# Gated linear attention into a SwiGLU feed-forward block: the input layout of one early attention unit, the queue of three loads, and the places of two weight sums

## The chip, the cores and the metric

The kernel runs on one core of a Trainium2 chip. The core has a matrix engine (TensorE, PE in the profile), a vector engine (VectorE, DVE), an engine for functions of one operand (ScalarE, ACT), GpSimd (POOL) and SyncE (SP), which mostly issues transfers. The engines run their own instruction streams in order and wait for each other by semaphores. Transfers go through 16 DMA engines; the queue of SP and that of GpSimd both feed them. The metric is the device time of one execution in microseconds (us), as the median of some runs.

## What is computed

Inputs q, k, v and f_logit have the shape (4, 8, 768, 48): batch, heads, sequence, head dimension. All is float32. The first part is a recurrence over the sequence, for each batch and head:

```
f = 1 / (1 + exp(-f_logit))
state = 0                                     # 48 x 48
for t in range(768):
    state = f[t][:, None] * state + outer(k[t], v[t])
    y[t]  = q[t] @ state
```

The result is put together to 3072 tokens of 384 features (8 heads of 48), and goes through a feed-forward block with a hidden width of 1536:

```
g   = x @ w_gate
out = (g * sigmoid(g) * (x @ w_val)) @ w_out
```

## The kernel before

**Chunks and units.** The sequence is cut into 6 chunks of 128 steps. A unit is one chunk of one batch element, all 8 heads; unit u = 4c + b is chunk c of batch element b, so that units 4 to 7 are chunk 1. In a unit the recurrence becomes matrix work: VectorE forms running products of the gates, forward and backward (two scans, lines 620 and 648), and multiplies k and q by them (line 570, `kT` and `qT`); PE forms the scores (`sc`, line 666), VectorE masks them (line 681), PE forms the output `y` (lines 702 and 706, or 727) and the state's increment `dS` (line 747). `attention(u)` is a Python generator; each `next` emits the next step.

**Two ways to bring in f, k and q.** All three are needed with the head dimension on the partitions and time along the row, and are stored the other way round.
- By TensorE: one DMA of 192 KB for each of f, k, q puts time on the partitions (`raw`, line 454, SP's queue), and PE turns it by four transposes of 128x128 each (`transposed`, line 587). ScalarE reads f from PSUM with the sigmoid, VectorE reads k and q from PSUM in the multiplications.
- By squares: four DMAs of 96 KB each lay the tensor out in squares of 32x32 (`rooms`, line 447), ScalarE applies the sigmoid to f in SBUF (line 595), and VectorE turns f, k and q by one STREAM_TRANSPOSE each (lines 604, 614 and 652). PE does nothing for these. In chunk 1 the rooms are the same memory as the two slots of `raw`; there is one room each for f, k and q, so the next unit's f is loaded when this unit's f has been turned, and so on (`load_after`).

`by_squares(u)` decides. Here it holds for the last two units of chunk 1 (6 and 7) and all of the later chunks. In chunk 1 the square loads are issued from GpSimd's queue, in a fixed order (`by_pool`); in later chunks from SP's.

**Feed-forward work.** While the attention of chunk 1 runs, the feed-forward block of chunk 0 runs in its plain form (`mlp_plain`): products of 128x512 with w_gate and w_val, and then the product with w_out (`downs_abreast`, line 825). Beside it the weights, which are stored with 64-bit floats, come in by 768 KB pieces and are made into float32 (`sizes` on ScalarE, lines 488 and 490; `join` on VectorE, lines 496 to 501). From chunk 1 on the feed-forward block uses forms with fewer products: for the first two products (`mlp_fifteen`) a triple of tiles takes 15 products in place of 18 (line 1004; four triples a chunk), and for the product with w_out (`down_seven`) seven block products in place of eight (lines 1103 and 1166). VectorE adds and subtracts the results (lines 905 and 908) and forms the hidden values h (line 956). These forms need sums of weights beforehand. Those of w_out's halves are four instructions of 128x1152 on VectorE (`down_weight_sums`, line 936), of which the first two give the operands `ws`.

**What sets the order.** The main order is that in which the Python code emits instructions. Up to line 1271 it is fixed engine by engine (`in_order`); between there and line 1292 the tile framework's scheduler may move instructions, so that attention, weights and products of chunk 0 are mixed by it; from line 1298 on the order is fixed again, and steps of attention and weight sums are put in by a written clock: each product counts 0.86, each part of the product with w_out 1.95, and an entry of `waiting` comes when the clock `now` has passed its number. `DOWN_SUMS_AT` (line 901) holds the numbers of the four sums of w_out's halves; `whole`, the length of chunk 1 on that clock, is 78.9. The first sum of the four is read by the second, the second by the fourth.

**The step that loads unit 5.** Before, line 1268 (`load(B + 1)`) issues the 192 KB loads of f, k, q and v of unit 5 on SP's queue, between pieces of the weights. For unit 6 the load is issued within the attention of unit 5, when PE's transposes of k and q have been emitted (line 628).

Of the kernel before, what the change touches and what calls it, by code (L numbers as in the profile page):

```python
# [290 lines left out]
def short_path(ctx, tc, ident, least, judge, q, k, v, f_logit, moe_w_gate, moe_w_val, moe_w_out, out):  # L291
# [9 lines left out]
    nc = tc.nc  # L301
    B, H, S, D = q.shape
# [13 lines left out]
    SQUARES = 2  # L316
# [82 lines left out]
    rooms = {nm: t.rearrange("p n h w -> p (n h w)")[:, 0:Q + HP * RUN] for nm, t in both_raw.items()}  # L399

    def by_squares(u):
        return u >= SQUARES * B - 2

    def make_rooms(pool):
        for nm in "fkq":
# [3 lines left out]
    def v_of(u):  # L409
        return vs[u % (NV if units[u][1] < SQUARES else NV // 2)]  # L410
# [20 lines left out]
    def load(u, what="fkqv"):  # L431
        b, c = units[u]
        rows = slice(c * C, (c + 1) * C)
        inputs = dict(f=f_logit, k=k, q=q, v=v)
        for nm in "fqkv" if c >= SQUARES else "fvkq" if by_squares(u) else "fkqv":
            src = inputs[nm]
            if nm not in what:
                continue
            if nm == "v":
                dst = v_of(u)  # L440
            elif not by_squares(u):
                dst = raw[nm][u % NRAW]
            else:
                since = len(traced)
                for n in range(4):
                    at = Q * (1 - n % 2)
                    (nc.sync if c >= SQUARES else nc.gpsimd).dma_start(
                        out=rooms[nm][Q * n:Q * (n + 1), at:at + HP * RUN].rearrange("t (a e) -> t a e", a=HP),
                        in_=src[b, n // 2::2, rows, :].rearrange("a (t i) d -> t a (i d)", i=NI))
                if c < SQUARES:  # L450
                    by_pool.extend(ins for ins in traced[since:] if ins.engine == mybir.EngineType.Pool)
                    keep_order(by_pool[-5:])
                continue
            nc.sync.dma_start(out=dst[:, :, 0:D], in_=src[b, :, rows, :].rearrange("h t d -> t h d"))

    def weight_piece(dst, src, parts):

# [97 lines left out]
    def attention(u):  # L555
# [4 lines left out]

        diagonal = None
        in_squares = by_squares(u)

        def multiply(out, x, by):
# [60 lines left out]
        if not in_squares:  # L625
            kp = transposed("kTp", kr)
            qp = transposed("qTp", qr)
            if by_squares(u + 1):
                load(u + 1)
# [120 lines left out]
        if c >= SQUARES and u + 2 < len(units):  # L750
            load(u + 2, "v")
# [7 lines left out]
    def load_after(u, what):  # L759

        if u + 1 < len(units) and u + 1 != SQUARES * B:
            load(u + 1, what)
# [16 lines left out]
    def keep_order(mine):  # L779
        for a, b in zip(mine, mine[1:]):  # L780
            tc.add_manual_dep(b, a.name, mybir.DependencyInfo(mybir.DependencyClass.NoSync,
                                                              mybir.DependencyReason.DATA), reason="order")
# [115 lines left out]
        return {"o": banks_o, "A": banks_a}[kind].tile([128, 512], FP32, tag=kind, name="sc")  # L898

    FINISH = (3, 5, 6, 7, 9, 10)  # L900
    DOWN_SUMS_AT = (28, 34, 38, 48)
    sums = {}

    def plus(dst, a, b):
# [31 lines left out]
    def down_weight_sums():  # L936

        DH = DM // 2
        b11, b12 = w_out[:, 0:NP, 0:DH], w_out[:, 0:NP, DH:DM]
        b21, b22 = w_out[:, NP:NF, 0:DH], w_out[:, NP:NF, DH:DM]  # L940
        for i in (1, 2, 4):
            down_sums[i] = comb.tile([128, NP, DH], FP32, tag=f"ws{i}", name=f"ws{i}")
        return [lambda: minus(down_sums[1], b12, b11), lambda: minus(down_sums[2], b22, down_sums[1]),
                lambda: minus(b12, b22, b12), lambda: minus(down_sums[4], b21, down_sums[2])]
# [256 lines left out]
    def weights():  # L1201
        if fetches:
            fetches.pop(0)()
        if sizes:
            sizes.pop(0)()
        if joins:
            joins.pop(0)()
# [57 lines left out]
    joins.pop(0)()  # L1265
    hidden[1]()
    weights()
    load(B + 1)
    hidden[2]()
    steps.pop(0)()  # L1270
    in_order(mark, (mybir.EngineType.PE, mybir.EngineType.DVE, mybir.EngineType.Activation, mybir.EngineType.SP))
# [37 lines left out]

    waiting += [(at, f) for at, f in zip(DOWN_SUMS_AT, down_weight_sums())]  # L1310
    blocks = {}
# [26 lines left out]
def kernel(  # L1338
# [22 lines left out]
    def judge(bank):  # L1361
# [13 lines left out]
        yield  # L1375

    short_path(tc, ident, least, judge, *args)
    with tc.If(redo[0] > 0, label="redo"):
        general_path(tc, *args)
# [32 lines left out]
```

## Time and profile before

| | |
|---|---|
| median of 3 runs | 604.13 us (604.05 to 604.21) |
| the profiled execution's own time | 605.36 us |
| its span, from the first to the last instruction | 603.5 us |
| TensorE's mean granted clock | 0.995 |
| PE busy | 591.9 us, 98% |
| DVE busy | 480.3 us, 80% |
| ACT busy | 294.8 us, 49% |
| POOL busy | 86.2 us, 14% |

Busy time of a PE whose matmuls are pipelined is not work at its peak; where PE really waits is seen in the waits and in the distance between successive groups of the timeline. In the timeline a group's first number is its start and its second its length, and lengths of neighbouring groups overlap a little. The stages in the profile: attention of chunk 0 up to 30 us; plain feed-forward of chunk 0 with the attention of chunk 1 from 30 to 143 us; then five blocks of four triples and a product with w_out, the first of them from 143 to 240 us.

### The profile page before, as it was taken

What the parts mean: (1) busy time and instruction counts of PE and PEld (TensorE: products, weight loads), DVE (VectorE), ACT (ScalarE), POOL (GpSimd) and SP (SyncE); (2) the same over time, 40 slices, a digit from 0 to 9 for tenths busy, and PEclk for the clock granted to TensorE, in tenths of its full rate; (3) what the DMA queues carried; (4) which work ended last, traced back from release to release, by engine and by line L of the source; (5) the groups of instructions that cost most, each with busy time, mean ns of one, the idle gap of its engine ahead of it and who ended that gap; (6) DMA issues with size and microseconds to landing.
All of it is one profiled execution on the core that took longest, in us unless ns stands there. A gap on an engine that the chain in (4) does not pass through costs nothing.

```text
span 603.5 us, 10851 instructions
## 1 busy us (share of the span) xinstructions
PE 591.9 (98%) x4004; PEld 487.6 (81%) x4004; DVE 480.3 (80%) x831; ACT 294.8 (49%) x559; POOL 86.2 (14%) x199
## 2 busy tenths in 40 slices
PE   7899999999999999999999999999999999999996
PEld 5754545667888899888899888899988899988896
DVE  7999997868999977998895978995878982666631
ACT  2577853215776521567631476742376730356600
POOL 1001251000030150030330030330030320000000
PEclk9999999999999999999999999999999999999999
DMA  9998682015322044342434333343240100100001
GB/s 197 243 294 286 199 211 63 5 35 157 80 63 69 17 129 124 102 114 65 115 103 109 116 91 71 87 110 101 85 105 26 28 9 6 53 1 1 1 1 55
DMA packets 105210, 56.28 MB, mean 93 GB/s; under 512 B 67136, under 2 KB 97216, under 8 KB 105152
## 3 DMA queue, kind: packets, MB, share of 16 engines
q1 hardware_dynamic: 97632, 46.49, 29.4%
q0 software_dynamic: 5504, 6.30, 3.5%
q10 hardware_dynamic: 2016, 2.75, 1.3%
q8 instruction: 32, 0.52, 0.4%
q14 instruction: 26, 0.21, 0.1%
HBM read 45.74 MB, written 6.82 MB: 87 GB/s over the span
## 4 chain that ended last, share of the span: by engine, by line
PE 93%; DVE 5%; issue 1%; ACT 0%; DVEq 0%; ACTq 0%
PE o L1103 19%; PE A L1004 16%; PE B L1004 13%; PE c L1004 5%; PE o L1004 5%; PE gate L802 5%; PE o L825 5%; PE val L802 5%; PE sc L666 4%; PE o L1166 3%; PE y L706 3%; PE y L727 2%; PE dS L747 2%; PE y L702 2%; PE kt L670 1%; DVE c L908 1%
## 5 line engine op out<-in xcount | busy, mean ns | idle before, releaser
L717 POOL DMA_DIRECT2D xT<-yT x120 | 59.9, 507 | 50.3 <-ACT yT L710 45.3
L1103 PE MATMUL o<-w_out,h 128*128 128x192 f32 x360 | 62.0, 327 | 0.5 <-DVE h L956 0.5
L1004 PE MATMUL A<-xs,w_both 128*128 128x256 f32 x240 | 62.2, 382 | 0.0
L1103 PEld LDWEIGHTS o<-w_out,h 128*128 128x128 f32 x360 | 58.7, 190 | 1.7 <-DVE h L956 0.8
L1009 ACT COPY c<-A 128x512 f32<-128x512 f32 x40 | 23.3, 583 | 59.5 <-PE A L1004 59.5
L1009 ACT COPY aside<-A 128x512 f32<-128x512 f32 x60 | 35.1, 586 | 33.7 <-PE A L1004 33.6
L905 DVE TENSOR_TENSOR c<-c,aside 128x512 f32<-128x512 f32 x60 | 41.1, 685 | 12.4 <-ACT aside L1009 11.0
L1004 PEld LDWEIGHTS A<-xs,w_both 128*128 128x128 f32 x240 | 44.9, 190 | 6.6
L956 DVE TENSOR_TENSOR h<-h,c 128x256 f32<-128x256 f32 x100 | 40.4, 412 | 7.3 <-ACT h L1020 7.1
L681 DVE TENSOR_TENSOR A<-sc,causal 128x512 f32<-128x512 f32 x48 | 30.9, 686 | 16.9 <-PE sc L666 16.9
L908 DVE TENSOR_TENSOR c<-c,aside 128x512 f32<-128x512 f32 x60 | 40.9, 682 | 2.8 <-ACT aside L1009 2.8
L1020 ACT ACTIVATE h<-c 128x256 f32<-128x256 f32 x100 | 39.2, 416 | 7.6 <-DVE c L905 5.7
L656 POOL MEMSET gates<- 128x4 f32 x24 | 3.3, 139 | 272.6 <-DVE qT L570 267.5
L1103 PE MATMUL o<-ws,h 128*128 128x192 f32 x240 | 41.5, 328 | 0.2 <-DVE A L681 0.2
L1004 PE MATMUL B<-xs,w_both 128*128 128x256 f32 x160 | 41.3, 380 | 0.1
L1004 PE MATMUL c<-xT,w_both 128*128 128x256 f32 x160 | 41.2, 380 | 0.1
L1004 PE MATMUL A<-xs,extra 128*128 128x256 f32 x160 | 41.2, 380 | 0.0
L1004 PE MATMUL B<-xT,extra 128*128 128x256 f32 x160 | 41.1, 379 | 0.0
L1009 ACT COPY aside<-B 128x512 f32<-128x512 f32 x60 | 35.1, 585 | 9.5 <-PE B L1004 6.6
L1103 PEld LDWEIGHTS o<-ws,h 128*128 128x128 f32 x240 | 39.1, 190 | 0.8 <-DVE A L681 0.4
L905 DVE TENSOR_TENSOR c<-c,o 128x384 f32<-128x384 f32 x15 | 8.3, 552 | 36.3 <-PE o L1103 36.3
L908 DVE TENSOR_TENSOR c<-o,c 128x512 f32<-128x512 f32 x40 | 27.4, 684 | 11.0 <-ACT h L1020 6.2
(149 smaller groups left out, 1221.0 us busy)
## 6 DMA issues: line engine op xcount, KB each, us to landing
fsquares<-in_f_logit_dram SPq DMA_DIRECT2D x64, 96.0 KB, 2.5
qsquares<-in_q_dram SPq DMA_DIRECT2D x64, 96.0 KB, 2.1
ksquares<-in_k_dram SPq DMA_DIRECT2D x64, 96.0 KB, 2.4
v<-in_v_dram SPq DMA_DIRECT2D x24, 192.0 KB, 2.7
w<-in_moe_w_gate_dram SPq DMA_DIRECT2D x6, 768.0 KB, 6.1
w<-in_moe_w_val_dram SPq DMA_DIRECT2D x6, 768.0 KB, 6.2
w<-in_moe_w_out_dram SPq DMA_DIRECT2D x6, 768.0 KB, 5.6
out_dram<-ob ACTq DMA_DIRECT2D x14, 192.0 KB, 2.0
```

Of the source, the lines that this page charges most:

```text
L666: nc.tensor.matmul(sc[par][:, a * C:(a + 1) * C], lhsT=kT[r, a, :], rhs=qT[r, a, :], start=True, stop=True)
L681: nc.vector.tensor_tensor(A[:, par], sc[par].rearrange("p (a t) -> p a t", t=C), causal.unsqueeze(1).broadcast_to((128, HP, C)), ALU.mult)
L717: (nc.gpsimd if c >= SQUARES else nc.sync).dma_start(out=xT[c][f % 128:f % 128 + n, f // 128, b * C:(b + 1) * C], in_=yT[r:r + n, par, a / ...
L802: nc.tensor.matmul(p, lhsT=w[:, j, i, :], rhs=xT[c][:, i, :], start=(i == 0), stop=(i == KT - 1))
L825: nc.tensor.matmul(p, lhsT=hidden_tile(h, n // 2)[:, n % 2 * 2 + b // 2, b % 2 * C:(b % 2 + 1) * C], rhs=w_out[:, j, :], start=(n == 0), s ...
L905: nc.vector.tensor_tensor(dst, a, b, ALU.add)
L908: nc.vector.tensor_tensor(dst, a, b, ALU.subtract)
L956: lagging.append(lambda: f(*args))
L1004: nc.tensor.matmul(p[name][:, n, :], lhsT=weights_of[a][:, n, j, :], rhs=tokens[b], start=fresh and n == 0, stop=True, skip_group_check=True)
L1009: nc.scalar.copy(t, p[name])
L1020: nc.scalar.activation(dst, src[:, 0, :], AF.Silu)
L1103: nc.tensor.matmul(p[:, n, :], lhsT=lhsTs[j][:, n * C:(n + 1) * C], rhs=rhs[:, j, :], start=first and j == order[0] and n == 0, stop=j == ...
```

## The change

Three edits:
- `by_squares` holds for unit 5 too, so that three of chunk 1's four units come in by squares. Line 1268 goes: unit 5's load is now issued within the attention of unit 4, when PE's transposes of its k and q have been emitted.
- In chunk 1 the loads of v for the units by squares (5, 6 and 7) are issued from GpSimd's queue in place of SP's.
- The first two of the sums of w_out's halves come at 13.1 and 26.5 on the written clock, in place of 28 and 34. The other two stay.

```diff
     def by_squares(u):
-        return u >= SQUARES * B - 2
+        return u >= SQUARES * B - 3
...
-            nc.sync.dma_start(out=dst[:, :, 0:D], in_=src[b, :, rows, :].rearrange("h t d -> t h d"))
+            queue = nc.gpsimd if c < SQUARES and by_squares(u) else nc.sync
+            queue.dma_start(out=dst[:, :, 0:D], in_=src[b, :, rows, :].rearrange("h t d -> t h d"))
...
-    DOWN_SUMS_AT = (28, 34, 38, 48)
+    DOWN_SUMS_AT = (13.1, 26.5, 38, 48)
...
     weights()
-    load(B + 1)
     hidden[2]()
```

SQUARES and B are 2 and 4. In the instruction streams of the changed kernel PE loses twelve transposes (four each of f, k and q of unit 5), VectorE gains three STREAM_TRANSPOSEs and has the two sums in other places, SP loses four loads of unit 5 and two of v, and GpSimd's stream is, for chunk 1: v of units 5, 6 and 7, then four loads each of f, k and q of unit 5, then of unit 6, then of unit 7, with the small memsets of line 656 between. ScalarE has unit 5's sigmoid on SBUF, right after the second SiLU of line 812, with a load of its function table before it and another for the next SiLU; its number of table loads is the same.

## The prediction

> **What bounds the kernel now.** I read the chain that ended last first, then PE's waits, then the timelines of PE, VectorE and ScalarE from 143 to 207 us, where the two moved sums lie, and from 30 to 143 us, where unit 5 lies.
>
> The page's chain:
>
> ```profile
> PE 93%; DVE 5%; issue 1%; ACT 0%; DVEq 0%; ACTq 0%
> ```
>
> PE sets the end nearly everywhere. An instruction taken from PE's stream is worth its full time if nothing else becomes late, and what PE waits for is the 5%. PE's waits over 143 to 240 us name VectorE twice:
>
> ```profile
> PE o L1103 <- DVE h L956: 0.5, 1, 0.5
> PE o L1103 <- DVE A L681: 0.2, 1, 0.2
> ```
>
> The list is not complete: small waits show only as a distance between starts. PE's timeline, start and length (lines left out):
>
> ```profile
> 174.68 1.03 PE L1004 MATMUL A<-xs,w_both 128*128 128x256 f32 x4
> ...
> 187.77 1.03 PE L1004 MATMUL A<-xs,w_both 128*128 128x256 f32 x4
> 188.91 1.13 PE L1004 MATMUL B<-xs,w_both 128*128 128x256 f32 x4
> ...
> 195.30 1.13 PE L1004 MATMUL c<-xT,w_both 128*128 128x256 f32 x4
> ...
> 201.59 2.76 PE L1103 MATMUL o<-w_out,h 128*128 128x192 f32 x16
> 204.90 1.57 PE L1103 MATMUL o<-w_out,h 128*128 128x192 f32 x8 [0.55 <-DVE h L956]
> 206.39 0.67 PE L702 MATMUL y<-qT,decayed 48*64 48x128 f32 x16
> ```
>
> Triple 3 takes 13.09 us (174.68 to 187.77), triple 4 takes 13.82 (to 201.59), the first part of the product with w_out 4.80 (to 206.39). In chunk 2, which has no w_out sums, the same pieces take 13.19 (287.31 to 300.50) and 3.90 (300.50 to 304.40). So PE loses 0.63 + 0.90 = about 1.5 us here. The chain says to whom: from 174.3 to 188.3 us it runs over VectorE, both moved sums in it.
>
> ```profile
> 172.20 0.68 DVE L905 TENSOR_TENSOR c<-c,aside 128x512 f32<-128x512 f32 x1
> 174.29 1.29 DVE L681 TENSOR_TENSOR A<-sc,causal 128x512 f32<-128x512 f32 x2 [1.41 <-PE sc L666]
> ...
> 176.15 1.35 DVE L908 TENSOR_TENSOR ws<-w_out 128x1152 f32<-128x1152 f32 x1
> ...
> 185.92 1.33 DVE L908 TENSOR_TENSOR ws<-w_out,ws 128x1152 f32<-128x1152 f32 x1
> ```
>
> VectorE idles 1.41 us before 174.29, then is full (31.34 of 32 us between 175 and 207), and ScalarE waits 1.53 us for it at 188.28.
>
> From 30 to 143 us PE has no wait. VectorE is nearly full up to 99 us, but early: its h multiplications (line 816) free the PSUM banks of `val` some 4.5 us or more before PE wants them, weight tiles are joined 5.8 us or more before their first product, and between 100 and 107 us it idles 1.03, 1.89 and 2.91 us.
>
> **What the Trainium skill says.** "DMA: Bandwidth & Descriptors", section "SWDGE vs HWDGE vs iDMA": loads from GpSimd have their descriptors built in software, into rings in SBUF that VectorE can lock GpSimd out of, and each DMA engine takes turns between the queues. The same page, "Anatomy of one DMA — SWDGE (gpsimd) path": about 2.0 us plus bytes/436e3 to landing, so 2.2 us for 96 KB, and many descriptors can be made before their cost shows. Here the f loads from GpSimd landed in a median of 6.7 us, k in 2.5: the estimate is right for quiet queues, wrong where weights stream. "Perfetto Trace Analysis", "DMA Instruction — SWDGE (GPSIMD)": the profile's end is when descriptors are written, not when data has landed; so I count landing apart. "ScalarE: Activation LUTs", "What ACT_TABLE_LOAD costs": 1283 ns a load; the trace has 1.28 us (the drain that the page adds is not separate in it).
>
> **The change, part by part.**
>
> *PE's transposes.* Twelve go: unit 5's fTp delays the next group from 57.25 to 57.69 (0.44), kTp and qTp from 72.83 to 73.71 (0.88). Sum 1.32 us, on the path. PE's stream around is otherwise the same.
>
> *VectorE's three transposes.* f 1.10 us (line 604), k and q 0.70 each (614, 652), less some 0.08 overlap each: 2.3 us more in 47 to 100 us. I added up the changed kernel's VectorE stream with the before row's steps (0.46 to 0.50 for a weight step, 0.87 for a join, 0.60 for a 128x512 sum, 1.14 a scan): unit 5's f is turned at about 50, its k at 56, q at 65; the `val` banks come free 4 to 9 us before they are wanted; VectorE reaches the last h multiplication at about 100.3, where PE, 1.32 us earlier than before, delivers at 102.1 to 102.4. So it is hidden, by the idle time at 100 to 107 us; without that cover it would cost 2.3 us.
>
> *ScalarE.* Same number of table loads. But the one for unit 5's sigmoid now stands in ScalarE's queue at 40.5 us, after the SiLU at 39.96, and waits for unit 5's f. Behind it: the copy `least`, the weight steps of the next piece, a table load, the SiLUs of gate tiles 2 and 3. When does f land? GpSimd's queue: v of unit 5 after dS of unit 1 and the memset at 20.34; v of unit 6 after dS at 24.6; v of unit 7 after dS of unit 3, 30.7; f after PE's fTp of unit 4, 34.1. Four f loads at 0.55 us (line 447) end at 36.4; landing 6.7 us later gives 43. A v load has 1024 pieces of 192 bytes against 128 of 768 in an f load; no row shows it from this queue. Bounds: 0.55 us (cost per DMA) to 4.4 us (eight times as many pieces). At 4.4, v of unit 7 ends at 35.1 and f lands at 44. I take the lower value; the difference is 1 us. With 43: sigmoid done at 44.9, weight step at 46.8, table and SiLU at 48.6, whose bank PE wants at 54.2. VectorE's next weight step needs ScalarE's at 46.8 and would come at 47.2 anyway. For unit 6, f is issued when unit 5's is turned (51), lands by about 60, ScalarE arrives at 59.3, SiLUs end near 63.5, bank wanted at 67.1. Cost 0. The cover is gone when unit 5's f lands after some 47 us; from there each us is a us on PE.
>
> *SP.* It loses six loads, so weight pieces are asked for up to 5 us earlier; they were early already. Worth 0, but they share the DMA engines with f (6.7 us rather than 2.2 is for that).
>
> *Unit 5's scores.* Before, its qT was ready 1.4 us before PE's `sc` at 78.95; now about 66.6 against 77.6. Worth 0.
>
> *The two sums.* In the changed order the first stands between the last c sum of triple 1's backlog (ends 157.09) and STREAM_TRANSPOSE f at 157.94, where VectorE idles 0.84 us; the second right before the mask at 174.29, in the idle 1.41. Each takes 1.27. The first pushes the rows behind it by about 0.43 until 172.9; ScalarE's copy of c at 166.23, which waits for an h of VectorE, leaves its bank 0.5 us before PE's product at 167.34, so PE loses 0 to 0.45, I take 0.1. The second fits, leaving the mask 0.2 late. After 176 VectorE has 2 x 1.27 = 2.5 us less to do, is 2.3 us earlier at the end of triple 3, and its inputs there (asides copied by 184 to 188 us) are ready that early. The h that PE waited for at 204.41 comes up to 2 us earlier against PE; 0.55 to 1 is needed. Gain: the 1.5 us lost in triple 4 and the part after it, of which 1.1 to 1.55 is plausible; I take 1.55. The wait at 221.96 (0.19, a mask) stays. The sum kept at 48 stays late in triple 4, but with 0.8 us of slack.
>
> *Sum.* 603.5 - 1.32 - 1.55 + 0.1 = 600.7 us of span. The profiled execution took 605.36 with 1.9 us around the span and 1.2 over the median; I carry the difference, 2.77 us, to the median: 604.13 - 2.77 = 601.4 us.
>
> **Rivals.**
> - *Only the transposes count.* VectorE stays behind in triples 3 and 4 since its backlog is remade by the table loads on ScalarE or by the sum at 48, or the first sum costs its 0.45. For it: VectorE is 98% busy there. Against: chunk 2 runs the same triple without loss. 604.13 - 1.32 to 604.13 - 1.6 + 0.45: about 602.8.
> - *VectorE becomes the bound before 103.* The 2.3 us are not absorbed, PE waits for banks at the start of the product with w_out. For: full up to 99 us. Against: 5.8 us idle after it. Loses up to 2.3: 601.4 + 2.3 = 603.7, no change.
> - *Slower: ScalarE stands at unit 5's f.* Mechanism: a load in GpSimd's queue behind v, in the time of the heaviest weight traffic (DMA share 0.92 between 30 and 57 us); ScalarE is in order, and weight steps and SiLUs wait behind. It decides from landing at 47 us: a landing at 52 costs 5 us: 601.4 + 5 = 606.4. For: landing times reached 7.8 us. Against: f would have to land 13 us after its issue at 34.1.
> - That the change doesn't do what it says is excluded by the instruction streams.
>
> **How the numbers follow.** The full gain 0.62, with its own range 600.9 to 602.2; only transposes 0.15 (602.2 to 603.4); VectorE bound 0.09 (603 to 604.5); slower 0.12 (605.4 up); more gain than reckoned 0.02. The measurement tells about 0.2%, 1.2 us: faster is under 602.92, slower over 605.34. Faster 0.62 + 0.02 + 0.6 of 0.15 and a rest = 0.75; same 0.13; slower 0.12. Range for 8 in 10: 600.7 to 604.0, which takes in the full gain, the transposes alone and half of VectorE's case.
>
> **What would show it.** Right: the first product of chunk 1 (143.03 before) starts at 141.7; ScalarE's wait for f ends before 45 us; triple 4 takes 13.1 to 13.2 us and the part after it 3.9; no `ws` between 176 and 190 us. Wrong: a PE wait for ScalarE's SiLU or for VectorE's h between 54 and 106 us; a triple 2 longer than 13.36 us by more than 0.2; v loads of several us in GpSimd's rows.

## The result: 602.3 us, and where it differs from the forecast

The changed kernel takes 602.3 us in the median (601.79 to 604.62), the kernel before 604.11 us measured beside it (603.92 to 604.30). The ratio is 0.9977, 95% interval 0.9970 to 0.9983. So it is faster by 1.8 us, where 601.4 us, faster by 2.77, were forecast. The profiled execution took 602.8 us, its span is 601.1 us.

The page's chain after the change; shares of the span by engine. They add up to 86% because the chain is followed back only to 82.5 us:

```profile
PE 84%; DVE 2%; ACT 0%; issue 0%; DVEq 0%; ACTq 0%
```

PE's waits from 25 to 240 us of the changed kernel (us in total, times, longest):

```profile
PE y L728 <- ACT kt L680: 1.0, 1, 1.0
PE gate L803 <- ACT h L813: 0.9, 1, 0.9
...
PE o L1104 <- DVE A L682: 0.2, 1, 0.2
```

The 0.5 us for VectorE's `h` in the product with w_out are gone. The row for a SiLU of ScalarE is new, and the 1.0 us at `y` were 0.6 in the kernel before. Both cost time between 25 and 92 us, the stage that was to give only a gain.

PE's timeline (start, length, line, operation) at the places that the prediction named. Lines of the changed kernel are numbered one higher here than the same lines before, and in some variants a few higher still:

```profile
141.68 1.03 PE L1005 MATMUL A<-xs,w_both 128*128 128x256 f32 x4
...
173.32 1.03 PE L1005 MATMUL A<-xs,w_both 128*128 128x256 f32 x4
...
186.41 1.03 PE L1005 MATMUL A<-xs,w_both 128*128 128x256 f32 x4
...
199.50 4.33 PE L1104 MATMUL o<-w_out,h 128*128 128x192 f32 x24
203.75 0.67 PE L703 MATMUL y<-qT,decayed 48*64 48x128 f32 x16
```

Triple 3 takes 13.09 us as before, triple 4 13.09 (before 13.82), the first part of the product with w_out 4.25 (before 4.80). The moved sums return 0.73 + 0.55 = 1.28 us. VectorE's timeline shows the four sums, and the idle time that is left beside them:

```profile
155.66 1.35 DVE L909 TENSOR_TENSOR ws<-w_out 128x1152 f32<-128x1152 f32 x1
171.64 1.34 DVE L909 TENSOR_TENSOR ws<-w_out,ws 128x1152 f32<-128x1152 f32 x1
176.18 0.69 DVE L909 TENSOR_TENSOR c<-o,c 128x512 f32<-128x512 f32 x1 [1.31 <-PE o L1005]
190.67 1.35 DVE L909 TENSOR_TENSOR w_out<-w_out 128x1152 f32<-128x1152 f32 x1
197.21 1.34 DVE L909 TENSOR_TENSOR ws<-w_out,ws 128x1152 f32<-128x1152 f32 x1
```

Chunk 1 starts at 141.68 us, as forecast (141.7), against 143.03. But that agreement is an accident. The profiled execution of before had something that is no part of the kernel: a dip of PE's clock just ahead of the chunk's first weights. Stretches 26 to 31 us of the two profiles (columns: stretch, length, busy time and instructions of PE, weight loads, VectorE, ScalarE, GpSimd, then PE's clock, DMA share, GB/s); the first line is of before, the second of after:

```profile
26.00:31.00 5.00, 4.36 (x65) 3.54 (x62) 4.86 (x12) 2.31 (x7) 0.00 (x0) 0.70 0.91 217
```

```profile
26.00:31.00 5.00, 3.97 (x67) 2.67 (x64) 4.83 (x12) 2.99 (x8) 0.73 (x2) 1.00 1.02 263
```

PE's mean clock is 0.70 in one and 1.00 in the other. By single microseconds the first isn't an even 0.70: the clock is 0.50 from 28 to 31 us and 0.81 over the next, so that it was halved for 3.4 us. One of these rows of before:

```profile
29.00:30.00 1.00, 1.00 (x21) 0.62 (x14) 0.97 (x3) 0.29 (x1) 0.00 (x0) 0.50 0.71 209
```

The dip comes in some executions, of the kernel before as of variants of both. The kernel with only the sums moved, below, shows what it costs: its profiled execution has the dip too (0.70) and took 604.03 us. Four of its 16 executions took 604.03 to 604.44 us at a mean clock of 0.996, the other twelve 602.67 to 603.01 at 0.998 or more. That is 1.3 us, and in the traces 1.35 (the first `val` product starts at 34.09 us in before, at 32.74 in a kernel without the dip and without the costs told below). It also accounts for the 1.2 us by which the profile of before lay over its median. Without it chunk 1 of the kernel before would start at 143.03 - 1.35 = 141.68 us. (The kernel with only v moved, below, agrees: no dip, PE 0.23 us late at 29.85 us, chunk 1 at 141.91.) So in this execution of the changed kernel nothing at all is left of the 1.32 us of transposes.

### The profile page after: what moved, and what is told of

It reads as the page before. It is cut to its first block, busy times and chain, and to the rows that moved or that the text cites. A ratio compares the mean times of both kernels' runs of the same rounds, so it can differ in the third digit from the quotient of the medians.

```text
span 601.1 us, 10842 instructions
## 1 busy us (share of the span) xinstructions
PE 588.2 (98%) x3992; PEld 484.8 (81%) x3992; DVE 482.1 (80%) x834; ACT 294.8 (49%) x559; POOL 95.3 (16%) x214
## 4 chain that ended last, share of the span: by engine, by line
PE 84%; DVE 2%; ACT 0%; issue 0%; DVEq 0%; ACTq 0%
PE o L1104 20%; PE A L1005 18%; PE B L1005 14%; PE o L1005 6%; PE c L1005 6%; PE o L826 5%; PE sc L667 3%; PE o L1167 3%; PE y L707 2%; PE y L728 1%; PE y L703 1%; PE dS L748 1%; PE gate L803 1%; PE val L803 1%; PE kt L671 0%; DVE A L682 0%
## 5 line engine op out<-in xcount | busy, mean ns | idle before, releaser
L1005 PEld LDWEIGHTS A<-xs,w_both 128*128 128x128 f32 x240 | 44.9, 190 | 6.6
```

Source lines behind the costliest of these rows:

```text
L1005: nc.tensor.matmul(p[name][:, n, :], lhsT=weights_of[a][:, n, j, :], rhs=tokens[b], start=fresh and n == 0, stop=True, skip_group_check=True)
```

## What took it: two rows of the trace

**A SiLU behind a weight step.** In chunk 0's feed-forward block PE forms the twelve `gate` tiles in order, after the first two in pairs, and the last pair (tiles 10 and 11) goes into PSUM banks that the SiLUs of tiles 8 and 9 have to free. PE's wait for the SiLU of tile 8 is called the wait at gate tile 8 below. PE at that place, and ScalarE's timeline ahead of it, in the changed kernel:

```profile
91.65 5.42 PE L803 MATMUL gate<-xT,w_both 128*128 128x512 f32 x12 [0.86 <-ACT h L813]
```

```profile
86.53 0.56 ACT L680 COPY kt<-kt 128x512 f32<-128x512 f32 x1
88.60 1.09 ACT L489 ACTIVATE up<-w 128x768 uint16<-128x768 uint32 x1 [1.50 <-DVE w_both L502]
89.70 1.28 ACT L813 ACT_TABLE_LOAD   x1
91.00 0.60 ACT L813 ACTIVATE h<-gate 128x512 f32<-128x512 f32 x1
```

ScalarE's weight step `up` of a w_out piece writes into a buffer that VectorE's join of w_both (87.61 to 88.56) frees. ScalarE is in order, so the table load and the SiLU of gate tile 8, whose bank PE wants at 90.79, stand behind it. The same rows of the kernel before:

```profile
86.87 1.08 ACT L488 ACTIVATE up<-w 128x768 uint16<-128x768 uint32 x1 [4.61 <-DVE w_both L501]
87.81 0.58 ACT L812 ACTIVATE h<-gate 128x512 f32<-128x512 f32 x1
```

The wait was there already and longer, 4.61 us. It cost nothing: the SiLU was done at 88.39 and PE wanted the bank at 93.01 (91.66 without the dip). In the changed kernel the join starts 1.72 us later (87.61 against 85.89), a table load of 1.28 us has come in between (unit 7's sigmoid now stands at 83.83, before the SiLUs of tiles 8 and 9, not at 92.74 behind them), and PE is there earlier.

**A v load that holds VectorE.** GpSimd's and VectorE's timelines of the changed kernel around the second moved v load, and PE's `y` behind them:

```profile
24.95 0.89 POOL L455 DMA_DIRECT2D v<-in_v_dram  x1 [2.90 <-PE dS L748]
```

```profile
25.27 0.73 DVE L497 TENSOR_SCALAR top<-top 128x384 f32<-128x384 f32 x1
...
27.40 1.28 DVE L682 TENSOR_TENSOR A<-sc,causal 128x512 f32<-128x512 f32 x2
```

```profile
28.19 1.21 PE L728 MATMUL y<-A,v 128*32 128x128 f32 x32 [1.02 <-ACT kt L680]
```

The same TENSOR_SCALAR and `y` in the kernel before (the length of `y` there is stretched by the dip):

```profile
25.27 0.35 DVE L496 TENSOR_SCALAR top<-top 128x384 f32<-128x384 f32 x1
```

```profile
27.80 1.84 PE L727 MATMUL y<-A,v 128*32 128x128 f32 x32 [0.64 <-issue]
```

In the changed kernel the step ends at 26.00, 0.16 us after GpSimd is done at 25.84. Everything behind it on VectorE is 0.38 us late, the mask A (now 27.40, before 27.02) too, and PE's `y`, which needs the mask, starts at 28.19 instead of 27.80. The profile puts PE's wait down to the copy of `kt`, but that had ended at 27.84; the other operand is the mask, in two instructions of 0.68 us, and the first ends at 28.08. The trace lists PE's weight load for this `y` among those that waited for the mask. The Trainium skill, "SBUF — State Buffer", section "Who interferes with whom", has the rule: VectorE in a 2-port mode and GpSimd share a pair of SBUF ports, and whoever starts first has them for the whole instruction while the other stands. `tensor_scalar` is among the operations it names as able to enter such a mode. The trace fits, if "whole instruction" is counted from a little after the start of GpSimd's row. At the third v load one VectorE step still gets through and the next is held:

```profile
30.31 0.90 POOL L455 DMA_DIRECT2D v<-in_v_dram  x1 [4.26 <-PE dS L748]
```

```profile
30.37 0.35 DVE L497 TENSOR_SCALAR top<-top 128x384 f32<-128x384 f32 x1
30.76 0.60 DVE L499 TENSOR_SCALAR top<-top 128x384 int32<-128x384 int32 x1
```

In all traces of this case 13 TENSOR_SCALAR steps are stretched beside a v load, and each ends 0.15 to 0.16 us after the load's row; a step that starts 0.05 or 0.06 us after the row's start takes its usual 0.35 us. Which mode a step ran in, the profile doesn't show.

## The experiments

The experiments ask three things: are the two parts of the change independent; does the v load cost what the two rows suggest; and is the SiLU's lateness that of VectorE's join. Lowest and highest times are given beside medians, since times of one kernel spread by up to 3 us: from the small margin at the SiLU, and from PE's clock.

**Only the sums moved** (the kernel before, no other edit):

```diff
-    DOWN_SUMS_AT = (28, 34, 38, 48)
+    DOWN_SUMS_AT = (13.1, 26.5, 38, 48)
```

> The kernel before with the two w_out sums moved and nothing else. Theory A (the change is two independent parts, and triple 4 and the part after it lost their time to the two sums): triple 4 takes 13.1 instead of 13.82 us, the first part of the product with w_out 4.25 instead of 4.80, chunk 1 starts as before (143.0), no wait of PE between 54 and 107 us; 1.28 us off, about 602.8. Rival B (the stalls go with VectorE's earlier arrival in chunk 1, that is with the transposes): triple 4 stays at 13.8 us and the time at about 604.1.

602.83 us (602.67 to 604.44), ratio 0.9982 (0.9975 to 0.9990). Triple 4 takes 13.08 us, the part after it 4.28, and PE's wait for `h` there is gone. Theory A holds: 1.28 us in the trace, 1.23 in the medians, come from the sums alone. That chunk 1 starts at 143.05 us, as expected, is again the dip, which this execution has as before had.

**Only the units** (the changed kernel with the sums where they were):

```diff
-    DOWN_SUMS_AT = (13.1, 26.5, 38, 48)
+    DOWN_SUMS_AT = (28, 34, 38, 48)
```

> The changed kernel with the sums where they stood before: unit 5 by squares and v from GpSimd's queue alone. Theory A: PE loses twelve transposes (1.32 us) and waits 0.86 us for a SiLU near 91.6, chunk 1 starts 0.46 us earlier than in the kernel before, triple 4 stays at 13.8 and the part after it at 4.8 us; about 603.65. Rival B (the stalls go with the transposes): triple 4 near 13.1 us and about 602.4. Rival C (no new wait here, the wait in the changed kernel is of the sums): about 602.8.

603.64 us (603.03 to 604.37), ratio 0.9991 (0.9982 to 0.9999). Triple 4 is back at 13.83 us, the wait of 0.55 for `h` too, and PE waits 0.48 us at gate tile 8. So unit 5 by squares, with v from GpSimd's queue, is worth 0.4 us in place of 1.32. The time is what theory A gave (603.65), but not for its reason: it counted one loss of 0.86 us, where the trace has two, 0.48 at gate tile 8 and 0.38 from the v load.

**All v loads back in SP's queue** (the changed kernel otherwise):

```diff
-            queue = nc.gpsimd if c < SQUARES and by_squares(u) else nc.sync
+            queue = nc.sync
```

> The changed kernel with its v loads put back in SP's queue; VectorE's and ScalarE's order as in the changed kernel. Theory A (the queue of the v loads is worth nothing): f of unit 5 lands at 43 to 44 us, the wait for the SiLU near 91.6 stays between 0.6 and 1.1 us, the time is that of the changed kernel (602.3) within 0.3. Rival D (the v loads share the DMA engines with f and weights from GpSimd's side, and make VectorE's weight steps late): f lands earlier, the SiLU's wait shrinks below 0.4 us, about 601.7.

601.25 us (601.10 to 601.39), ratio 0.9955 (0.9941 to 0.9968). Theory A is wrong here, by 1 us, and rival D right in direction: less waiting, and more gain than its 601.7. VectorE's step and PE's `y` in this kernel:

```profile
25.28 0.35 DVE L497 TENSOR_SCALAR top<-top 128x384 f32<-128x384 f32 x1
```

```profile
27.82 1.21 PE L728 MATMUL y<-A,v 128*32 128x128 f32 x32 [0.64 <-issue]
```

Row by row, VectorE in the changed kernel loses 0.38 us at 25.27, 0.24 at 30.76 (a TENSOR_SCALAR of 0.60 instead of 0.36 while the third v load is written, 30.31 to 31.21), 0.15 near 47, and 0.64 at 52.34 waiting for a weight piece; some of it is won back later: 1.3 us in sum at the join of w_both. ScalarE goes on with unit 5's f at 42.13 instead of 43.69. PE doesn't wait at gate tile 8, but only just: ScalarE still waits 1.49 us for the join, the SiLU is done at 90.29 us, and PE takes the bank at 90.34. Chunk 1 starts at 140.37, which is 141.68 less the 1.32 us of transposes. The median is 0.2 us below 604.06 - 1.32 - 1.28; that rest isn't accounted for.

**The SiLUs ahead of the weight step** (one order on ScalarE):

```diff
+    keep_order([silus[8], silus[9], ups[-3]])
```

`silus` and `ups` are the SiLUs by gate tile and the weight steps `up` in the order of the program.

> The changed kernel with one order changed on ScalarE: the table load and the SiLUs of gate tiles 8 and 9 stand before the weight step of the third piece of w_out, which waits for VectorE's join. Theory A (PE's new wait near 91.6 comes from this place: the weight step waits for VectorE, then a table load, then the SiLU): PE waits less than 0.1 us there, chunk 1 starts at 140.8 instead of 141.7 us; about 601.4. Rival E (VectorE as a whole is late, and any place in the queue only moves the wait): PE waits about as long, for VectorE's h multiplication or a weight tile between 91 and 107 us; 602.3.

602.40 us (601.91 to 603.46), ratio 0.9973 (0.9961 to 0.9985): no gain. ScalarE's row says why:

```profile
89.69 0.94 ACT L493 ACTIVATE top<-w 128x768 f32<-128x768 f32 x1 [1.51 <-DVE w_both L504]
```

Only `up` was held back; the step `top` of the same piece came to its place, with the same wait for the same join. The experiment didn't take the cause away, and PE still waited 0.44 us (in an execution that had the dip).

**v of unit 6 alone, and v of unit 7 alone, back in SP's queue:**

```diff
-            queue = nc.gpsimd if c < SQUARES and by_squares(u) else nc.sync
+            queue = nc.gpsimd if c < SQUARES and by_squares(u) and u != 6 else nc.sync
```

> The changed kernel with the v load of unit 6 alone back in SP's queue; units 5 and 7 stay on GpSimd. Theory P (while GpSimd writes the 1024 descriptors of a v load, from 24.95 to 25.84 us, VectorE's weight step at 25.27 can't finish: 0.73 us instead of 0.35, and the mask behind it, which PE waits for, is late by as much): the step takes 0.35 us, PE's first gate product starts at 29.6 instead of 30.0 us, the wait for the SiLU near 91 stays at 0.4 to 0.9; 0.38 us off, about 601.9. Rival Q (all that the queue costs comes from f of unit 5 landing late): first gate product at 30.0 us, about 602.3.

> The changed kernel with the v load of unit 7 alone back in SP's queue; units 5 and 6 stay on GpSimd. Theory P: the first gate product stays at 30.0 us; the weight step at 30.76 takes 0.36 instead of 0.60 us; f of unit 5, no longer behind the 1024 pieces of unit 7's v in the same queue, lets ScalarE go on before 43 us instead of 43.7; VectorE no longer stands at a weight at 52 us; the wait for the SiLU near 91 is under 0.3 us; about 601.65. Rival R (f's landing is set by the weights' traffic, not by v ahead of it): ScalarE goes on at 43.2 to 43.7, the wait stays at 0.4 to 0.9, about 602.3.

Unit 6: 601.93 us (601.35 to 603.24), ratio 0.9957 (0.9943 to 0.9971). Unit 7 (`u != 7`): 602.65 us (601.52 to 604.74), ratio 0.9974 (0.9965 to 0.9984). VectorE's two steps, first with unit 6's load away, then with unit 7's:

```profile
25.27 0.35 DVE L497 TENSOR_SCALAR top<-top 128x384 f32<-128x384 f32 x1
...
30.37 0.61 DVE L499 TENSOR_SCALAR top<-top 128x384 int32<-128x384 int32 x1
```

```profile
25.27 0.72 DVE L497 TENSOR_SCALAR top<-top 128x384 f32<-128x384 f32 x1
...
30.75 0.36 DVE L499 TENSOR_SCALAR top<-top 128x384 int32<-128x384 int32 x1
```

Each load stretches its own step and no other: theory P is shown for VectorE's steps. PE's first gate product starts at 29.61 us with unit 6's load away and at 30.00 with unit 7's away. With unit 7's away ScalarE goes on at 42.60 and PE has no wait in that trace, as theory P has it, but the median is 1 us over the 601.65 expected; four of the twenty executions, 604.33 to 604.74 us, ran at a mean clock of 0.993. With unit 6's away, in the profiled execution (603.24 us, the slowest of its times) VectorE stood 2.12 us for a gate weight and PE 0.69 us at gate tile 8. There ScalarE took unit 5's f at 41.84 us without waiting for it, though unit 7's v stood ahead of it. In the six traces with unit 7's v ahead the four f loads landed in a median of 6.2 to 7.6 us after their issue, in the five without in 5.6 to 7.0. So f may land later behind v, but the two overlap and it isn't shown; weights that land late are a source of delay that comes and goes between executions. The worth of unit 7's load can't be read from these medians; the lowest times, 601.35 and 601.52 against 601.79 of the changed kernel, only suggest 0.4 and 0.3.

**A second load ahead of v of unit 6**, 1024 pieces of 16 bytes into a spare tile that nothing reads:

```diff
+            if u == 6:
+                spare = att.tile([128, HP * 2, 4], FP32, tag="spare", name="spare")
+                queue.dma_start(out=spare[:], in_=src[b, :, rows, 0:4].rearrange("h t d -> t h d"))
```

> The changed kernel with one more load on GpSimd right ahead of v of unit 6: the same 1024 pieces of v, of 16 bytes each, into a spare tile that nothing reads. Theory P (descriptor writing holds VectorE's weight steps): VectorE's steps from 25.27 us on are held until both loads are written, about 26.7 us, 0.9 us longer than in the changed kernel; PE's first gate product starts at 30.9 us, about 603.2. Rival Q (the 0.38 us are chance, or come from v's bytes): the step stays at 0.73 us or less, the first gate product at 30.0, about 602.3.

605.53 us (604.48 to 606.76), ratio 1.0023 (1.0015 to 1.0031), but not for the reason expected. The spare tile waits for nothing, so the load went to the front of GpSimd's stream, among the first f, k and q. GpSimd's row, and PE's first transposes behind it:

```profile
3.23 1.05 POOL L457 DMA_DIRECT2D spare<-in_v_dram  x1
```

```profile
6.56 0.63 PE L594 MATMUL qTp<-idf,qraw 128*128 128x128 f32 x4 [0.59 <-DMA qraw<-in_q_dram]
8.01 0.77 PE L594 MATMUL fTp<-idf,fraw 128*128 128x128 f32 x4 [0.82 <-DMA fraw<-in_f_logit_dram]
```

This second fTp stands at 6.60 us in the changed kernel. The gate product starts 1.49 us later than there; VectorE's step beside v of unit 6 takes 0.70 us, as in the changed kernel. It tells nothing of two loads in a row. Nor is the 1.49 us simply the late loads. PE's clock is halved here from 8.4 to 11.8 us, right behind the two waits shown, and PE's filler products (`idle`) from 8.57 us take 2.77 us in place of 1.46. PE starts unit 0's `sc` at 11.27 us, in the changed kernel at 10.04, though VectorE's `qT`, which it needs, is no later (9.83 against 9.90). At full clock these products would have ended near 10.03 (8.57 + 1.46, an estimate). So 1.23 of the 1.49 us in this execution are the dip's, and the late loads alone would have cost PE next to nothing before `sc`. Two executions at a full mean clock (1.000) took 604.73 and 604.75 us; what they lost isn't shown.

**Only v moved** (the kernel before, v of units 6 and 7 from GpSimd):

```diff
-            nc.sync.dma_start(out=dst[:, :, 0:D], in_=src[b, :, rows, :].rearrange("h t d -> t h d"))
+            queue = nc.gpsimd if c < SQUARES and by_squares(u) else nc.sync
+            queue.dma_start(out=dst[:, :, 0:D], in_=src[b, :, rows, :].rearrange("h t d -> t h d"))
```

> The kernel before with the v loads of units 6 and 7 in GpSimd's queue, nothing else. Theory P (descriptor writing holds VectorE's weight step at 25.27 us, which PE feels): PE's gate starts 0.38 us later, everything else has slack here (in the kernel before the SiLU of gate tile 8 is ready 4.6 us before it is wanted): 604.05 + 0.38 = 604.4. Rival (it costs only in the changed kernel, or f lands later and PE waits for it): 604.05 without the first, over 604.8 with the second.

604.00 us (603.73 to 605.49) against 604.17, ratio 0.9996 (0.9987 to 1.0005). The expected 0.38 us isn't to be seen in the time; the interval, -0.8 to +0.3 us, leaves room for a little less. The trace has a hold, but a smaller one. GpSimd's and VectorE's rows:

```profile
24.94 1.16 POOL L455 DMA_DIRECT2D v<-in_v_dram  x1 [4.49 <-PE dS L748]
```

```profile
25.27 0.35 DVE L497 TENSOR_SCALAR top<-top 128x384 f32<-128x384 f32 x1
25.65 0.60 DVE L499 TENSOR_SCALAR top<-top 128x384 int32<-128x384 int32 x1
```

Here VectorE's first step got through, GpSimd's writing took 1.16 instead of 0.89 us, and VectorE's second step was held for 0.24; it ends 0.15 us after the load's row, as the others do. PE's first gate product starts at 29.85, 0.23 us after the 29.62 of the kernel with all v loads in SP's queue. VectorE's first step, 0.33 us after the start of the row, ran through from 25.27 to 25.62, and GpSimd's row is 0.27 us longer: this time GpSimd seems to have stood. In six other traces a step 0.32 to 0.34 us after the start of the row was held. So what is lost depends on which of the two comes first. PE doesn't wait at gate tile 8 in this kernel: the SiLU is done at 88.39 as in the kernel before.

**One join ahead, then both.** The first edit puts VectorE's second pair of weight sums, and with it the join of w_both that follows, ahead of the next join of w_out:

```diff
-        hidden.insert(hidden.index(weights, 3 * at), lambda n=n: behind(lambda: [t[n]() for t in sums_of]))
+        hidden.insert(hidden.index(weights, 3 * at), lambda n=n: behind(lambda: [t[n]() for t in sums_of]) if n != 1 else moved())
...
+    keep_order([joined[-6]] + mine)
```

`moved` issues the pair without tying it to the last VectorE instruction and keeps it in `mine`; `joined`, and below `masks` and `tops`, are the joins, masks and second weight steps in the order of the program.

> The changed kernel with VectorE's order alone changed: the second pair of weight sums (85.21 us) and the join of w_both behind it (87.61), whose buffer ScalarE's weight step at 88.60 waits for, stand some 6 us earlier, ahead of the next join of w_out. Same work on every engine. Theory V (PE's wait at gate tile 8 is the place of that join in VectorE's full queue): ScalarE's 1.5 us wait for the join goes, the SiLU ends before 90 us, PE doesn't wait there; chunk 1 starts at 140.8, the median goes to the changed kernel's lowest times, about 601.8, and the times lie closer together. Rival W (the wait comes from transfers that land late, f at 43 us and weights, whatever the order): PE still waits 0.4 us or more near 91 or somewhere between 91 and 107 us; about 602.3.

602.09 us (601.80 to 602.89), ratio 0.9967 (0.9955 to 0.9980), and PE still waits 0.51 us. ScalarE's step and VectorE's timeline of this kernel:

```profile
88.24 1.08 ACT L490 ACTIVATE up<-w 128x768 uint16<-128x768 uint32 x1 [1.84 <-issue]
```

```profile
82.04 0.95 DVE L503 CUSTOM_DVE_ANT_0 w_both<-top,up 128x1536 uint16<-128x1536 uint16 x1
...
87.20 0.95 DVE L503 CUSTOM_DVE_ANT_0 w_out<-top,up 128x1536 uint16<-128x1536 uint16 x1
```

The join of w_both is 5.6 us earlier, but in exchange the join of w_out stands at 87.20, and it frees the other buffer of ScalarE's steps. ScalarE's row starts 0.1 us after it ends. That the step waits for this join is inferred from the times; the profile names no releaser (`issue`). If so, the place had changed hands, and this run can't decide between V and W. The last edit adds the other join, and ScalarE's SiLUs ahead of `top`, on top of v in SP's queue and of the sums at (13.1, 26.5, 28, 38):

```diff
+    keep_order([joined[-5], masks[10]])
+    keep_order([silus[8], silus[9], tops[-3]])
```

> The version with the join ahead, v in SP's queue and the third and fourth sums moved, and besides: the join of w_out that ScalarE's weight step at 88.2 waits for there (87.2 to 88.2) stands ahead of the two masks, and ScalarE's SiLUs of gate tiles 8 and 9 ahead of the next step `top`. Theory V (what PE waits for at gate tile 8 is how late VectorE frees the buffer that ScalarE's weight step, in front of the SiLU, writes into, whichever join that is; putting one join ahead only made the other the last): ScalarE's step starts right behind its copy of kt, near 87, the SiLU ends 0.4 us or more before PE wants it; about 600.3, 0.5 below the version with one join ahead. Rival W (late transfers): about 600.8, with PE waiting somewhere between 91 and 107 us.

600.74 us (600.57 to 601.02), ratio 0.9942 (0.9928 to 0.9955). VectorE, ScalarE and PE there:

```profile
84.43 0.94 DVE L504 CUSTOM_DVE_ANT_0 w_out<-top,up 128x1536 uint16<-128x1536 uint16 x1
```

```profile
85.45 1.07 ACT L490 ACTIVATE up<-w 128x768 uint16<-128x768 uint32 x1
86.54 1.28 ACT L817 ACT_TABLE_LOAD   x1
87.83 1.09 ACT L817 ACTIVATE h<-gate 128x512 f32<-128x512 f32 x2
```

```profile
90.35 5.42 PE L807 MATMUL gate<-xT,w_both 128*128 128x512 f32 x12
```

The step no longer waits, and both SiLUs are done at 88.92, 1.4 us before PE wants the first bank. So theory V has the cause of the wait, as the trace shows. It doesn't have the time: 600.3 was expected, and the median is within 0.1 us of the version with one join ahead (600.82, next), whose executions can therefore have lost hardly anything at this place. Against the same kernel with no join ahead (601.27, next) the two are 0.53 and 0.45 us lower, with five or six executions each.

**The sums further on, and the three together:**

```diff
-    DOWN_SUMS_AT = (13.1, 26.5, 38, 48)
+    DOWN_SUMS_AT = (13.1, 26.5, 28, 38)
```

> The changed kernel with all v loads back in SP's queue, and the third and fourth w_out sums at 28 and 38 instead of 38 and 48: the third falls into the 1.3 us that VectorE idles before 176 us, the fourth takes the third's place. Theory (PE's rest in the first part of the product with w_out, 4.25 against 3.90 us in chunk 2, is the sum that stood at 197 us): triple 4 stays at 13.1, the part after it takes 3.9 us, about 600.9. Rival (the third sum makes the rows behind it late, or another row of VectorE takes over): triple 3 or 4 longer by 0.3 or more, 601.3 or above.

> Three things together: the join ahead, all v loads in SP's queue, the third and fourth w_out sums at 28 and 38. If each is worth what its own run showed (0 to 0.7 for the join, 0.38 for v of unit 6, 0.35 for the sums) and they don't share a cause: gate at 29.6 us, no wait near 91, first part of the product with w_out 3.9 us; about 600.75, the lowest of all kernels. If the join only moves the wait: 601.2 or above.

With v in SP's queue and these sums: 601.27 us (600.66 to 602.37), ratio 0.9948 (0.9933 to 0.9963). The part after triple 4 takes 3.99 us, so 0.26 of the 0.35 expected is there; but in the profiled execution PE waited 0.69 us at gate tile 8, and the median is that of the kernel without these sums. With the join ahead besides: 600.82 us (600.62 to 602.18), ratio 0.9944 (0.9930 to 0.9958), as expected; its profiled execution is the 602.18, with the dip, so its trace doesn't show where the others stood. The last three kernels of this section reach down to 600.57 to 600.66. The version with both joins ahead beats both kernels: 1.6 us under the changed kernel's median, 3.4 under the kernel before.

## Why the prediction was right, and where it was wrong

The direction is right and the time lies in the range; the likeliest value was 0.9 us too low. The range (600.7 to 604.0) holds because it takes in rivals: the time lies just outside the 600.9 to 602.2 that were given to the full gain. And one of the prediction's own signs of being wrong came true: PE waits for a SiLU between 54 and 106 us, at 91.65.

- **PE's transposes, 1.32 us.** Right: chunk 1 starts at 140.37 and 140.38 us in the two kernels without the side costs (all v loads in SP's queue; both joins ahead), against 141.68 in the kernel before without the dip.
- **The stalls in triple 4 and after it, 1.55 less 0.1.** The mechanism is right, shown by moving the sums alone; the size was 1.28. Triple 4 gave back 0.73, more than the 0.63 counted. The term that was too large is the part after triple 4: 0.90 was to come back, 0.55 did. "The sum kept at 48 stays late in triple 4, but with 0.8 us of slack" had no such slack; moving it and the third sum forward returned another 0.26. The first sum's push cost nothing to be seen (triple 2 takes 13.35 us).
- **"ScalarE ... Cost 0".** This is the step that failed. Its numbers for unit 5 were good: f 43 forecast and 43.69 found, sigmoid 44.9 and 44.99, SiLU 48.6 and 48.76. It followed gate tiles 2 to 5 and stopped. Tiles 8 and 9, where unit 7's sigmoid moves ahead of them and brings a table load, were not followed; "same number of table loads" was counted, not where they lie. PE waited 0.86 us for the bank of tile 8.
- **"VectorE ... hidden, by the idle time at 100 to 107 us".** Half wrong. VectorE did reach the last h multiplication in time (the pair starts at 102.26). But the step asked only what PE takes from VectorE. ScalarE takes buffers from VectorE's joins, and ScalarE's SiLU goes to PE. The row with 4.61 us of idle for `w_both`, right ahead of a SiLU, was in the profile of before.
- **The v load, bounds 0.55 to 4.4 us, the lower value taken.** The issue took 0.89 to 1.05 us, near the lower bound; that it delays f isn't shown (landing 6.2 to 7.6 us after issue with unit 7's load ahead, 5.6 to 7.0 without). What was left out is VectorE: 0.38 us straight to PE. The prediction quoted the skill for VectorE locking GpSimd out; it also goes the other way, as VectorE's step at 25.27 shows, and this was not priced.
- **The rivals.** "VectorE becomes the bound before 103" named the right engine and the wrong exit: the wait stands at 91, through ScalarE. "ScalarE stands at unit 5's f" happened (2.96 us of wait before 43.69), but f landed well before 47 and PE didn't feel it there.
- **The median as reference.** The 1.2 us between the profile of before and its median were carried along unexplained. They are a clock dip. The sum of the prediction is a difference and isn't harmed by it, but its first sign is: "starts at 141.7" was counted from a profile with the dip, and was met by the dip's absence with none of the gain. The kernels' own difference is smaller than that of the profiles (605.36 - 602.8 = 2.6 us against 1.8).

The sum with what was measured: 604.1 - 1.32 - 1.28 + 0.38 = 601.9 us, the changed kernel's lowest times (601.79 to 601.90). The median's further 0.4 us fit the wait at gate tile 8, found at 0.86 and 0.48 us in two traces. The three highest times (604.40 to 604.62) ran at a mean clock of 0.993, the lowest of this kernel; the 602.3 itself ran at 0.999 to 1.000. The kernel before took 605.27 us at 0.995 and 606.14 and 606.47 at 0.992. So a lower clock made these executions slow, by about as much as two dips would (2 x 1.3 us, an estimate); where in the kernel it fell, no trace shows.

## What to carry to other kernels

When work is added to a full engine, follow each of its results to every engine that takes something from it, buffers too, and follow that engine's queue to its last result before the idle time that is to hide the work: a long wait on a helper engine right ahead of a result for the bound engine is the slack being spent. A load with many small pieces, issued from GpSimd, can cost VectorE time as well as GpSimd (here 1024 pieces, 0.24 to 0.38 us); look at which VectorE steps it meets. And before two profiles are subtracted, compare PE's clock stretch by stretch and each profile with its own median.

## What the runs showed of the hardware that was not expected

- While GpSimd writes the descriptors of a v load of 1024 pieces (rows of 0.88 to 1.16 us), one of VectorE's TENSOR_SCALAR steps of 128x384 takes 0.60 to 0.73 instead of 0.35 us. It ends 0.15 to 0.16 us after the load's row in all 13 cases, so it seems to be held until the load is written rather than slowed. A step that starts within 0.06 us of the row's start gets through (30.37 us in the changed kernel). Other operations keep their time: a TENSOR_TENSOR from PSUM started during the first v load (21.00 to 22.05) takes its usual 1.29 for two. Beside the f loads of 128 pieces the largest stretch seen is 0.12 us (0.68 instead of 0.56).
- In 4 of the 14 traces PE's clock is halved (0.50) for 3.4 us, from about 28.0 to 31.4 us (28.5 to 31.9 in one of them), which costs 1.3 us; in a fifth, that of the second load ahead of v, from 8.4 to 11.8. The Trainium skill, "TensorE: Matmul & The Clock Gate", section "What's actually happening", tells of a gate that follows PE's recent activity over a free-running window of some 3.4 us. The length of all five dips agrees with that window, and PE pauses 0.6 to 1.0 us ahead of each. What sets a dip off was not tested: PE pauses 0.64 us at 27.80 in the kernel before, with the dip, and 0.64 us at 27.82 with all v loads in SP's queue, without it.
